# A 16-point transform stage between matmuls: spectrum copied in three pieces, one store buffer more, pauses at block borders, and a weight chunk loaded earlier

## The chip, the cores and the metric

The kernel runs on one core of a Trainium2 chip. Its time is that of one execution on the device, in microseconds (us). TensorE multiplies matrices into PSUM banks, ScalarE and VectorE copy and combine what is there, GpSimd and SyncE mostly issue transfers (DMAs). Each engine works through its own instructions strictly in order.

## What is computed

Four layers run one after the other on a residual x of 2048 rows (S) and 576 channels (D); A mixes by two DFT matrices, B multiplies by a long convolution:

```python
def _A_ref(x, dft_seq_re, dft_seq_im, dft_hid_re, dft_hid_im):
    a = jnp.einsum("bsd,ed->bse", x, dft_hid_re)
    b = jnp.einsum("bsd,ed->bse", x, dft_hid_im)
    return jnp.einsum("ts,bse->bte", dft_seq_re, a) - jnp.einsum("ts,bse->bte", dft_seq_im, b)

def _B_ref(q, k, v, shift_k, ssm_k, ssm_D):
    ...
    kv = k_shift * v                      # k after a causal convolution of 4 taps
    kv_f = rfft(kv padded to 2 * S)       # per channel
    kf_f = rfft(ssm_k padded to 2 * S)
    y = irfft(kv_f * kf_f)[:S]
    return q * (y + kv * ssm_D)

x = x + _A_ref(_layernorm(x), A_dft_...)
x = x + _B_ref(_layernorm(x), B_k, B_v, B_shift_k, B_ssm_k, B_ssm_D)
x = x + _A_ref(_layernorm(x), A_dft_...)
x = x + _B_ref(_layernorm(x), B_k, B_v, B_shift_k, B_ssm_k, B_ssm_D)
```

In B only q depends on x. The convolution result y is the same in both B layers, so the kernel computes it once, beside the first A layer.

## The kernel before

All products are in fp32r. Each operand is split into a rounded high part (ScalarE, a copy) and the rest (VectorE, a subtraction); a product is three matmuls, high x high, high x low and low x high. This pair of instructions is `split` (L91 to L93), and most of the work of ScalarE and VectorE consists of it.

**The first A layer** is `layer` (L292) with 128 steps n: 4 blocks of 512 output rows, in each the real and the imaginary DFT, in each 16 steps k over the rows. A step has 14 matmuls of 512 columns: twelve into four accumulators s and two into a fifth, rm. The DFT matrix for it is loaded two steps ahead on SyncE and split into `cs` (the lines "mats<-flts 128x512" of L92 and L93). At the last k of sixteen, a border, the accumulators are copied out and split into the spectrum u (`evac_u`, `evac_r`). There is one set of accumulators, so the next step's matmuls wait for these copies. At n = 47, 79 and 111 the layer also yields `None` while products of the block before are pending.

**The hidden product** (`hidden`, L268) multiplies the spectrum of a finished block with the hidden DFT matrix W: 27 matmuls of 288 columns, released from their bank by a VectorE addition (L279). W has nine chunks of rows, loaded and split by `load_w` (L217) from step 41 on, two chunks to a step; the ninth has 64 rows of the real and 64 of the imaginary matrix with unlike signs. The first hidden product needs the ninth chunk last.

**The branch** (`branch`, L339) computes the convolution as a long transform in three stages. The middle one, the 16-point stage, has 64 groups. A group's feed is loaded from memory (`flts<-t`) and split (the "mid<-flts 128x576" lines); then come:

- `mid_kernel`: the transform of the convolution kernel, three matmuls into a bank. Partitions 0 to 63 hold the real part, 64 to 127 the imaginary part. ScalarE makes the buffer kk of two halves from it: one copy out of the bank (L496), then three copies of 64 partitions within SBUF (L497 to L499) that put real and imaginary part where the product needs them, one with its sign turned.
- `mid_signal`: the transform of the signal into another bank, and on VectorE the complex product of the two, with the half products in L505, L506 and L507 and their sum in L508. L507 is the last to read the signal's bank.
- `mid_round`: the split of the product (ScalarE "mid<-flts 128x288" and VectorE L492).
- `mid_inverse`, two groups later: three matmuls into a bank, a copy to a store buffer `vo`, a store.

ScalarE's copies of the stage all go through `act` (L483), so the page shows them under one line, L486; the VectorE half of the feed's and the round's split is L492. The last stage of the branch (`i2_products`) reads what the inverse stored, multiplies by a table i2c that GpSimd loads, and stores the result from the same `vo` buffers. All banks of the branch and of the hidden products are three buffers called bk.

**What sets the order.** The program is written as generators that the loop at L733 advances: after each half step of the layer (`whole` False, then True) it takes up to GROUPS = 2 yields of the branch as long as its share of the work is due. Where the work is behind, two yields follow every half step until it has caught up. Within that, the Tile framework's scheduler decides the order of the instructions on each engine and the bank that a product gets. At n = MID_LOAD (44, second half) the branch is advanced once: it lays out the stage's buffers and issues the first two feed loads. The stage's groups run from n = 47 to 103, the last stage's products to 111.

Of the kernel before, what the change touches and what calls it, by code (L numbers as in the profile page):

```python
# [10 lines left out]
F32 = mybir.dt.float32  # L11
FR = mybir.dt.float32r
AF = mybir.ActivationFunctionType
# [20 lines left out]
W_FROM = 41  # L34
HOLD = 125
W_SAVE = 60
MID_LOAD = 44
MID_FROM = 47
I2_END = 111
PREP = 113  # L40
# [25 lines left out]
def fnet_h3_kernel(ctx: ExitStack, tc: tile.TileContext, x, c_mat, w_re, w_im, k_pad, v, shift_k,  # L66
# [24 lines left out]
    def split(h, l, src):  # L91
        a = nc.scalar.activation(h, src, AF.Copy).ins  # L92
        return a, nc.vector.tensor_tensor(l, src, h.bitcast(F32), OP.subtract).ins  # L93

    @contextmanager
    def behind(*instructions):
        with ExitStack() as stack:
            for i in instructions:
                stack.enter_context(tc.issue_after(i))
            yield  # L100

    def split_in(h, l):

        split(h, l, l.bitcast(F32))
# [44 lines left out]

    flts = flat(FLT, F32, "flts")  # L150
    mhalf = flts[:, :1]
    lay(flts, 8, ("stat", STAT, 4))
    lay(flts, RT_AT, ("rt", NT, 1))
    lay(mats, X_END, ("cs", WIDE, 3))
# [9 lines left out]
            nc.gpsimd.dma_start(dst, src)  # L164

    nc.vector.memset(mhalf, -0.5)
    nc.scalar.activation(flts[:, 1:2], mhalf, AF.Copy)

    def norm_stats(src):
# [47 lines left out]
    def load_w():  # L217
        lay(flts, SC_AT + CRAW * NT + 4 * D, ("wl", D, 3))
        wg = region_a(FR, "w").rearrange("p (k n) -> p k n", k=9)
        for ch in range(9):  # L220
            w = two(wg[:, ch])
            raw = ring["wl"]()
            if ch < 8:
                nc.sync.dma_start(raw, (w_re if ch < 4 else w_im)[(ch % 4) * P:(ch % 4 + 1) * P, :])
            else:
                nc.sync.dma_start(raw[:REM], w_re[NC * P:, :])
                nc.sync.dma_start(raw[REM:], w_im[NC * P:, :])
            for lo, hi, sg in ((0, P, 1 if ch < 4 else -1),) if ch < 8 else ((0, REM, 1), (REM, P, -1)):
                if sg > 0:
                    split(w[lo:hi, 0, :], w[lo:hi, 1, :], raw[lo:hi])  # L230
                else:
                    nc.scalar.activation(w[lo:hi, 0, :], raw[lo:hi], AF.Copy, scale=-1.0)
                    nc.vector.scalar_tensor_tensor(w[lo:hi, 1, :], raw[lo:hi], -1.0,
                                                   w[lo:hi, 0, :].bitcast(F32), op0=OP.mult,
                                                   op1=OP.subtract)
            W.append(w)
            yield
        for ch in range(9):
            load_after(w_d[ch], wg[:, ch].bitcast(F32))
            yield  # L240
# [98 lines left out]
    def branch():  # L339
# [126 lines left out]
        at = lay(m1, at, ("yf", D, 2))  # L466
        lay(m1, at, ("fc", 4 * P, 2))
        at = lay(flts, SC_AT + CRAW * NT, ("res", D, 2))
        lay(flts, at, ("land", D, 2), ("kk", D, 2), ("vo", HD, 3), ("p2", HD, 1))
        mc = quads(ring["mc"]())  # L470
        load_fr(mc, midc)
        lo, hi = slice(0, 64), slice(64, 128)
# [10 lines left out]
        def act(*args, **kw):  # L483
            if last_act:
                with tc.issue_after(last_act[-1]):
                    last_act.append(nc.scalar.activation(*args, **kw).ins)  # L486
            else:
                last_act.append(nc.scalar.activation(*args, **kw).ins)
# [4 lines left out]

        def mid_kernel(df):
            pk, kk = mid_half(df, HD), two(ring["kk"]())
            act(kk[:, 0, :], pk[:, :HD], AF.Copy)  # L496
            act(kk[lo, 1, :], kk[hi, 0, :], AF.Copy)  # L497
            act(kk[hi, 1, :], kk[hi, 0, :], AF.Copy, scale=-1.0)
            act(kk[hi, 0, :], kk[lo, 0, :], AF.Copy)  # L499
            return kk  # L500

        def mid_signal(df, kk):
            px = mid_half(df, 0)
            p1, p2 = kk[:, 0, :], ring["p2"]()
            nc.vector.tensor_tensor(p1, px[:, :HD], p1, OP.mult)  # L505
            nc.vector.tensor_tensor(p2[lo], px[hi, :HD], kk[hi, 1, :], OP.mult)  # L506
            nc.vector.tensor_tensor(p2[hi], px[lo, :HD], kk[lo, 1, :], OP.mult)  # L507
            nc.vector.tensor_tensor(p1, p1, p2, OP.add)  # L508
            return p1

# [222 lines left out]
    for n, whole in layer(get_x0, lambda j: x[:, j, :], done0, pending):  # L733
        if (whole or whole is not None and n % J < J - 1) and n <= F1_END:
            at = n if whole else n - 0.5
            at16 = 4 + 2 * F1_16
            want = int(4 + F1_16 * at / 8 if at <= 16 else at16 + (68 - at16) * (at - 16) / (F1_END - 16))
            with behind(made[min(n + 2, J - 1)], *evac):
                while used < want:
                    next(br)  # L740
                    used += 1
        if whole is not None and n >= W_FROM and len(W) < 9:
            with behind(*stored):
                next(wl)
        if whole and n == MID_LOAD:
            next(br)
        if n >= MID_FROM:
            if whole is not None:
                passed += STEP * (4 if whole else 3) / 7 * BORDER.get(n % J, 1.05)
            if whole is None or whole and n % 2 == 1 and n % (2 * J) < J - 1 and pending:  # L750
                finish(pending, 1)
                passed += PIECE
            for _ in range(GROUPS):
                if spent < work * min(1.0, passed / total):
                    with behind(*added, *evac):
                        spent += next(br, work)
# [129 lines left out]
        HU[tb, ch] = t  # L886

    def split_u(tb, ch):
        t = HU[tb, ch]
        for lo, hi, sg in ((0, P, 1 if ch < 4 else -1),) if ch < 8 else ((0, REM, 1), (REM, P, -1)):  # L890
            h, l = t[lo:hi, 0, :], t[lo:hi, 1, :]
            if sg > 0:
                split_in(h, l)
            else:
                raw = l.bitcast(F32)
                nc.scalar.activation(h, raw, AF.Copy, scale=-1.0)
                nc.vector.scalar_tensor_tensor(l, raw, -1.0, h.bitcast(F32), op0=OP.mult, op1=OP.subtract)

    steps = [(tb, m, kp) for tb in range(1, TB) for m in ORDER for kp in range(KP)]
    cs, done = {}, []  # L900
# [205 lines left out]
```

## Time and profile before

| | |
|---|---|
| time, median of 3 runs | 1205.02 us (1201.5, 1205.02 and 1205.65) |
| profiled execution | 1202.6 us, its span on the core 1200.8 us |
| TensorE busy, weight loads busy | 98%, 85% of the span |
| VectorE, ScalarE, GpSimd busy | 70%, 55%, 6% |
| granted TensorE clock | 0.999 |
| DMA | 261.95 MB, 218 GB/s on average |

A row of the profile names the line, the engine, the operation, what it writes and reads, its shape and count, then its busy time in us, the mean in ns of one, and the idle time of the engine just before it with what ended that. PE is TensorE, PEld its weight load, which runs beside the matmul before; DVE is VectorE, ACT ScalarE, POOL GpSimd, SP SyncE. A busy TensorE is not TensorE at its peak, since the ends of matmuls are modelled. In a row of the timeline the first number is the start in us from the span's start, the second the duration.

### The profile page before, as it was taken

How to read it: one execution, taken by the hardware profiler on the slowest of the kernel's cores; microseconds unless marked ns; L12 is line 12 of the kernel's file. 1: busy time of each engine (PE TensorE's matmuls, PEld its weight loads, DVE VectorE, ACT ScalarE, POOL GpSimd, SP SyncE). 2: the span in 40 equal slices, each digit the busy share in tenths (PEclk: the TensorE clock that was granted, in tenths of full speed). 3: DMA queues.
4: the chain of work that ended last, by engine and by line, in shares of the span. 5: the costliest groups of instructions: out<-in, count | busy, mean ns of one | idle time of the engine just before them, and what ended most of it. 6: DMA issues, size and time to landing. Idle time of an engine off the chain costs nothing.

```text
span 1200.8 us, 18269 instructions
## 1 busy us (share of the span) xinstructions
PE 1177.3 (98%) x6320; PEld 1026.5 (85%) x6320; DVE 840.2 (70%) x1498; ACT 665.9 (55%) x1335; POOL 75.3 (6%) x116
## 2 busy tenths in 40 slices
PE   7999999999999999999999999999999999999997
PEld 6878888988888888888988898888888888889997
DVE  7889883679877677675346766775776777774764
ACT  7855665579866678675435566544444445550210
POOL 2210000000000000001101111000000000001111
PEclk9999999999999999999999999999999999999999
DMA  9779898546756667647967686872682677795621
GB/s 363 265 240 311 284 296 259 167 138 182 227 186 183 201 179 227 189 143 235 308 201 242 214 259 218 271 262 77 204 288 79 196 285 266 231 351 148 218 91 40
DMA packets 146110, 261.95 MB, mean 218 GB/s; under 512 B 15841, under 2 KB 44769, under 8 KB 146018
## 3 DMA queue, kind: packets, MB, share of 16 engines
q1 hardware_dynamic: 102674, 205.58, 53.5%
q10 hardware_dynamic: 36432, 42.63, 10.2%
q0 software_dynamic: 6912, 12.59, 4.1%
q8 instruction: 49, 0.80, 0.3%
q14 instruction: 43, 0.35, 0.1%
HBM read 194.09 MB, written 66.65 MB: 217 GB/s over the span
## 4 chain that ended last, share of the span: by engine, by line
PE 80%; ACT 6%; DVE 6%; DMA 4%; issue 2%; POOL 1%; ACTq 0%; SPq 0%; POOLq 0%; DVEq 0%
PE s L75 45%; PE bk L75 30%; PE rm L75 4%; ACT flts L486 3%; DMA flts<-in_c_mat 1%; ACT mid L486 1%; DVE mats L93 1%; DMA flts<-vd 1%; DVE mats L190 1%; DMA t<-flts 1%; ACT mats L92 1%; DMA mid<-in_i2c 1%; DVE f1f L387 1%; POOL flts L616 0%; DVE f1f L382 0%
## 5 line engine op out<-in xcount | busy, mean ns | idle before, releaser
L75 PE MATMUL s<-mats 128*128 128x512 f32 x2088 | 528.5, 391 | 0.8 <-DVE u L93 0.8
L75 PEld LDWEIGHTS s<-mats 128*128 128x128 f32 x2088 | 381.1, 188 | 71.0 <-DVE u L93 1.7
L93 DVE TENSOR_TENSOR mats<-flts,mats 128x512 fp32r<-128x512 f32 x206 | 141.0, 688 | 53.1 <-ACT mats L92 51.5
L92 ACT ACTIVATE mats<-flts 128x512 fp32r<-128x512 f32 x206 | 128.3, 627 | 85.1 <-PE bk L75 31.7
L75 PE MATMUL bk<-mid 128*128 128x288 f32 x768 | 128.1, 298 | 5.3 <-ACT flts L486 2.0
L75 PEld LDWEIGHTS bk<-mid 128*128 128x128 f32 x768 | 114.7, 188 | 20.5 <-ACT flts L486 5.6
L492 DVE TENSOR_TENSOR mid<-flts,mid 128x576 fp32r<-128x576 f32 (+1 forms) x160 | 101.9, 638 | 41.3 <-ACT mid L486 34.4
L75 PE MATMUL bk<-w,u 128*128 128x288 f32 x864 | 121.2, 296 | 1.1 <-DVE flts L279 0.6
L75 PEld LDWEIGHTS bk<-w,u 128*128 128x128 f32 x864 | 117.2, 188 | 5.4 <-DVE flts L279 1.5
L486 ACT ACTIVATE flts<-bk 128x288 f32<-128x288 f32 x160 | 63.0, 405 | 90.6 <-PE bk L75 71.6
L75 PE MATMUL rm<-mats 128*128 128x512 f32 x304 | 95.4, 390 | 0.0
L486 ACT ACTIVATE mid<-flts 128x576 fp32r<-128x576 f32 (+1 forms) x159 | 87.4, 582 | 10.8 <-DMA flts<-vd 7.0
L486 ACT ACTIVATE flts<-flts 64x288 f32<-64x288 f32 x192 | 85.0, 443 | 5.2
L432 ACT ACTIVATE flts<-bk 128x288 f32<-128x288 f32 x128 | 49.5, 410 | 46.4 <-PE bk L75 40.9
L75 PE MATMUL bk<-f1r 128*128 128x288 f32 x384 | 65.0, 301 | 8.1 <-ACT f1r L92 7.7
L75 PEld LDWEIGHTS bk<-f1r 128*128 128x128 f32 x384 | 59.3, 191 | 15.8 <-ACT f1r L92 8.5
L75 PE MATMUL bk<-mats 128*128 128x288 f32 (+1 forms) x376 | 67.8, 317 | 0.0
L75 PEld LDWEIGHTS rm<-mats 128*128 128x128 f32 x304 | 56.9, 188 | 11.8
L75 PE MATMUL s<-t,mats 128*128 128x512 f32 x264 | 64.9, 389 | 0.0
L176 POOL TENSOR_TENSOR flts<-flts 128x1 f32<-128x1 f32 x35 | 29.6, 846 | 523.3 <-DVE flts L175 523.3
L279 DVE TENSOR_TENSOR flts<-flts,bk 128x288 f32<-128x288 f32 x48 | 21.7, 453 | 57.4 <-PE bk L75 57.4
L75 PE MATMUL bk<-mats,t 128*128 128x288 f32 (+1 forms) x368 | 59.3, 303 | 0.0
(143 smaller groups left out, 1491.3 us busy)
## 6 DMA issues: line engine op xcount, KB each, us to landing
flts<-in_c_mat SPq DMA_DIRECT2D x148, 256.0 KB, 3.5
ph<-in_c_mat SPq DMA_DIRECT2D x54, 512.0 KB, 4.1
t<-flts ACTq DMA_DIRECT2D x64, 288.0 KB, 4.5
flts<-t SPq DMA_DIRECT2D x64, 288.0 KB, 3.0
flts<-in_c_mat SPq DMA_DIRECT2D x30, 512.0 KB, 5.2
vd<-flts ACTq DMA_DIRECT2D x64, 144.0 KB, 2.6
flts<-vd SPq DMA_DIRECT2D x32, 288.0 KB, 4.4
mid<-in_i2c POOLq DMA_DIRECT2D x32, 256.0 KB, 5.5
```

The lines of the kernel that those rows point to most:

```text
L75: nc.tensor.matmul(ps, lhsT, rhs, start=first, stop=last, skip_group_check=more)
L92: a = nc.scalar.activation(h, src, AF.Copy).ins
L93: return a, nc.vector.tensor_tensor(l, src, h.bitcast(F32), OP.subtract).ins
L176: pows.append(nc.gpsimd.tensor_tensor(rs, ve, mhalf, OP.pow).ins)
L190: made.append(nc.vector.tensor_tensor(t[:, D + REM:], y[:, :NC * P], h[:, :NC * P], OP.subtract).ins)
L279: added[:] = [nc.vector.tensor_tensor(r[:, cs], r[:, cs], ps[:, :HD], OP.add).ins]
L387: nc.vector.tensor_tensor(rp, rp, out_t, OP.add)
L432: stored[:] = [nc.scalar.activation(so[:, c, :], ps[:, :HD], AF.Copy).ins]
L486: last_act.append(nc.scalar.activation(*args, **kw).ins)
L492: nc.vector.tensor_tensor(l, src, h.bitcast(F32), OP.subtract)
```

## The change

Six edits:

- `mid_kernel` makes kk by three copies of 64 partitions out of the bank, each to its place, and leaves the sign to `mid_signal`. Before it was one copy out of the bank and three within SBUF.
- `mid_signal` writes the crossed half products into the second half of kk instead of a buffer of their own (p2). The first of them is now a three-operand instruction that turns the sign.
- The space of p2 becomes a fourth `vo` buffer.
- In the second half of step n with n % 16 = 14 and the first half of the next, no yield of the branch is taken.
- MID_LOAD is 45: the first feeds are requested behind the ninth chunk of W.
- The chunks with unlike signs (the ninth of W, the ninth of u in the last stage) are split by one pair of instructions over 128 partitions, with a column of +1 and -1 as the scale; before it took two pairs over 64. Two memsets at the start fill that column.

```diff
-MID_LOAD = 44
+MID_LOAD = 45
...
+    def signed_split(h, l, src, sign):
+
+        nc.scalar.activation(h, src, AF.Copy, scale=sign)
+        nc.vector.scalar_tensor_tensor(l, src, sign, h.bitcast(F32), op0=OP.mult, op1=OP.subtract)
...
+    nc.vector.memset(mixed[:REM], 1.0)
+    nc.vector.memset(mixed[REM:], -1.0)
...
-            for lo, hi, sg in ((0, P, 1 if ch < 4 else -1),) if ch < 8 else ((0, REM, 1), (REM, P, -1)):
...
+            if ch < 4:
+                split(w[:, 0, :], w[:, 1, :], raw)
+            else:
+                signed_split(w[:, 0, :], w[:, 1, :], raw, -1.0 if ch < 8 else mixed)
...
-        lay(flts, at, ("land", D, 2), ("kk", D, 2), ("vo", HD, 3), ("p2", HD, 1))
+        lay(flts, at, ("land", D, 2), ("kk", D, 2), ("vo", HD, 4))
...
-            act(kk[:, 0, :], pk[:, :HD], AF.Copy)
-            act(kk[lo, 1, :], kk[hi, 0, :], AF.Copy)
-            act(kk[hi, 1, :], kk[hi, 0, :], AF.Copy, scale=-1.0)
-            act(kk[hi, 0, :], kk[lo, 0, :], AF.Copy)
+            act(kk[lo, 0, :], pk[lo, :HD], AF.Copy)
+            act(kk[hi, 0, :], pk[lo, :HD], AF.Copy)
+            act(kk[hi, 1, :], pk[hi, :HD], AF.Copy)
...
-            p1, p2 = kk[:, 0, :], ring["p2"]()
+            p1, p2 = kk[:, 0, :], kk[:, 1, :]
             nc.vector.tensor_tensor(p1, px[:, :HD], p1, OP.mult)
-            nc.vector.tensor_tensor(p2[lo], px[hi, :HD], kk[hi, 1, :], OP.mult)
-            nc.vector.tensor_tensor(p2[hi], px[lo, :HD], kk[lo, 1, :], OP.mult)
+            nc.vector.scalar_tensor_tensor(p2[lo], px[hi, :HD], -1.0, p2[hi], op0=OP.mult, op1=OP.mult)
+            nc.vector.tensor_tensor(p2[hi], px[lo, :HD], p2[hi], OP.mult)
...
-            for _ in range(GROUPS):
+            near = whole and n % J == J - 2 or whole is False and n % J == J - 1
+            for _ in range(0 if near else GROUPS):
```

The order of the instructions changes from the ninth chunk of W on. TensorE's matmuls before its first hidden product and after the last product of the 16-point stage stand as before.

SyncE's loads around the ninth chunk, before (in_w_re and in_w_im are W, the 64x576 pair its ninth chunk; in_c_mat is the DFT matrix, t_75 a feed, in_x the residual):

```order
L160 DMA flts<-t_75 128x576
L224 DMA flts<-in_w_im 128x576
L160 DMA flts<-in_c_mat 128x512
L224 DMA flts<-in_w_im 128x576
L160 DMA flts<-t_75 128x576
L160 DMA flts<-in_c_mat 128x512
L226 DMA flts<-in_w_re 64x576
L227 DMA flts<-in_w_im 64x576
```

and now, with t_77 the feed:

```order
L166 DMA flts<-t_77 128x576
L232 DMA flts<-in_w_im 128x576
L166 DMA flts<-in_c_mat 128x512
L232 DMA flts<-in_w_im 128x576
L234 DMA flts<-in_w_re 64x576
L235 DMA flts<-in_w_im 64x576
L166 DMA flts<-t_77 128x576
```

The ninth chunk stands ahead of the second feed; the second DFT load of these rows has moved further up, out of this piece.

VectorE in two groups of the 16-point stage behind the first border, before (bk is a bank, 128x288 into mid the round's split, 128x576 the feed's):

```order
L505 TENSOR_TENSOR flts<-bk,flts 128x288
L506 TENSOR_TENSOR flts<-bk,flts 64x288
L507 TENSOR_TENSOR flts<-bk,flts 64x288
L492 TENSOR_TENSOR mid<-flts,mid 128x576
L508 TENSOR_TENSOR flts<-flts 128x288
L93 TENSOR_TENSOR mats<-flts,mats 128x512
L505 TENSOR_TENSOR flts<-bk,flts 128x288
L492 TENSOR_TENSOR mid<-flts,mid 128x288
L506 TENSOR_TENSOR flts<-bk,flts 64x288
L507 TENSOR_TENSOR flts<-bk,flts 64x288
L492 TENSOR_TENSOR mid<-flts,mid 128x576
```

and now:

```order
L508 TENSOR_TENSOR flts<-bk,flts 128x288
L509 SCALAR_TENSOR_TENSOR flts<-bk,flts 64x288
L496 TENSOR_TENSOR mid<-flts,mid 128x288
L510 TENSOR_TENSOR flts<-bk,flts 64x288
L496 TENSOR_TENSOR mid<-flts,mid 128x576
L511 TENSOR_TENSOR flts<-flts 128x288
L93 TENSOR_TENSOR mats<-flts,mats 128x512
L508 TENSOR_TENSOR flts<-bk,flts 128x288
L496 TENSOR_TENSOR mid<-flts,mid 128x288
L509 SCALAR_TENSOR_TENSOR flts<-bk,flts 64x288
L496 TENSOR_TENSOR mid<-flts,mid 128x576
L510 TENSOR_TENSOR flts<-bk,flts 64x288
```

The round's split stands between the half products in both; in the second group the feed's split now stands ahead of the last half product (L510, formerly L507), which is the last to read the signal's bank.

TensorE at the border at n = 79, from the hidden product on, before (w,u is the hidden product, mid the branch, s and rm the layer):

```order
L75 MATMUL bk<-w,u 128x288 x27
L75 MATMUL bk<-mid 128x288 x6
L75 MATMUL s_66<-mats 128x512
L75 MATMUL bk<-mid 128x288 x9
L75 MATMUL s_66<-mats 128x512 x2
L75 MATMUL s_67<-mats 128x512 x3
L75 MATMUL bk<-mid 128x288 x3
L75 MATMUL s_68<-mats 128x512 x2
L75 MATMUL bk<-mid 128x288
L75 MATMUL s_68<-mats 128x512
L75 MATMUL s_69<-mats 128x512 x3
```

and now:

```order
L75 MATMUL bk<-w,u 128x288 x27
L75 MATMUL bk<-mid 128x288 x9
L75 MATMUL s_66<-mats 128x512 x2
L75 MATMUL bk<-mid 128x288 x3
L75 MATMUL s_66<-mats 128x512
L75 MATMUL s_67<-mats 128x512 x3
L75 MATMUL s_68<-mats 128x512 x3
L75 MATMUL s_69<-mats 128x512 x3
L75 MATMUL rm<-mats 128x512 x2
```

Branch matmuls no longer stand between the layer's matmuls in the second part of the step; they follow behind the border.

More of the change, by code (lines that the diff above doesn't have):

```diff
@@ L151, in fnet_h3_kernel @@
     mhalf = flts[:, :1]
+    mixed = flts[:, 2:3]
     lay(flts, 8, ("stat", STAT, 4))
@@ L227, in load_w @@
                 nc.sync.dma_start(raw[REM:], w_im[NC * P:, :])
-            for lo, hi, sg in ((0, P, 1 if ch < 4 else -1),) if ch < 8 else ((0, REM, 1), (REM, P, -1)):
[L229 to L235, printed above, removed]
+            if ch < 4:
+                split(w[:, 0, :], w[:, 1, :], raw)
+            else:
+                signed_split(w[:, 0, :], w[:, 1, :], raw, -1.0 if ch < 8 else mixed)
             W.append(w)
@@ L888, in split_u @@
     def split_u(tb, ch):
[L889 to L897, printed above, removed]
+        h, l = HU[tb, ch][:, 0, :], HU[tb, ch][:, 1, :]
+        if ch < 4:
+            split_in(h, l)
+        else:
+            signed_split(h, l, l.bitcast(F32), -1.0 if ch < 8 else mixed)
     steps = [(tb, m, kp) for tb in range(1, TB) for m in ORDER for kp in range(KP)]
```

## The prediction, made before the changed kernel was run

> **What bounds the kernel now.** I read the stretches first, since the change touches one of them, then who waited for whom in it. The columns are the stretch, its length and the busy time of TensorE, its weight loads, VectorE, ScalarE and GpSimd, with their instructions in brackets.
>
> ```profile
> 214.00:441.00 227.00, 223.86 (x1315) 198.72 (x1314) 169.88 (x336) 167.88 (x366) 2.12 (x4) 1.00 0.60 181
> 441.00:617.00 176.00, 172.50 (x973) 151.74 (x972) 108.33 (x197) 111.54 (x238) 13.79 (x26) 1.00 0.71 217
> ```
>
> TensorE is busy for 223.86 of 227 us and for 172.50 of 176. The 16-point stage lies in these 403 us, and the change moves matmuls nowhere else and takes none away. A gain can come only out of TensorE's stalls here. The waits of the weight loads (PEld), then of the matmuls (PE), over the same 403 us (total, times, longest):
>
> ```profile
> PEld bk L75 <- ACT flts L486: 6.9, 16, 1.3
> PEld bk L75 <- DVE flts L507: 3.7, 7, 0.9
> PEld bk L75 <- DVE flts L279: 2.1, 4, 0.7
> PEld bk L75 <- DVE w L233: 0.7, 1, 0.7
> PEld s L75 <- DVE u L93: 0.7, 1, 0.7
> PEld bk L75 <- DVE mid L492: 0.4, 2, 0.2
> ```
>
> ```profile
> PE bk L75 <- ACT flts L486: 2.0, 4, 0.9
> PE bk L75 <- DMA mid<-in_i2c: 1.7, 1, 1.7
> PE bk L75 <- DVE flts L507: 1.3, 4, 0.4
> PE bk L75 <- DVE flts L279: 0.9, 3, 0.4
> PE bk L75 <- DVE w L233: 0.5, 1, 0.5
> PE s L75 <- DVE u L93: 0.2, 1, 0.2
> ```
>
> Without the wait for the i2c load, the weight loads waited 14.5 us and the matmuls 4.9. Neither is what TensorE lost: a load runs ahead of its matmul, and a late matmul still counts some waiting as busy. One stall gives the scale:
>
> ```profile
> 371.97 1.53 PE L75 MATMUL s<-mats 128*128 128x512 f32 x6
> 373.34 0.62 PE L75 MATMUL rm<-mats 128*128 128x512 f32 x2
> 374.58 1.53 PE L75 MATMUL s<-mats 128*128 128x512 f32 x6
> 376.56 0.82 PEld L75 LDWEIGHTS bk<-mid 128*128 128x128 f32 x6 [0.87 <-ACT flts L486]
> 376.56 1.06 PE L75 MATMUL bk<-mid 128*128 128x288 f32 x6 [0.45 <-ACT flts L486]
> ```
>
> Six layer matmuls undisturbed take 371.97 to 373.34, 1.37 us to the next start; the same six before the stall take 374.58 to 376.56, 1.98. So 0.61 was lost where PEld says 0.87 and PE 0.45. With 0.61/0.87 = 0.70 the 14.5 become 10.2 us; with 0.61/0.45 = 1.36 the 4.9 become 6.7. Many waits show on the loads alone, so I take 10.2. That is all the change can win; the i2c wait (1.7) is outside it, since its load waits for products whose order near there is unchanged. The span can't fall below about 1190.
>
> **The change, part by part.** *Spectrum pieces.* Costs on ScalarE and VectorE (busy, mean ns):
>
> ```profile
> L486 ACT ACTIVATE flts<-flts 64x288 f32<-64x288 f32 x192 | 85.0, 443 | 5.2
> L486 ACT ACTIVATE flts<-bk 128x288 f32<-128x288 f32 x160 | 63.0, 405 | 90.6 <-PE bk L75 71.6 <-ACT flts L486 5.0 <-DMA yb<-flts 4.7
> L486 ACT ACTIVATE mid<-flts 128x288 fp32r<-128x288 f32 x64 | 28.5, 445 | 1.7 <-DVE flts L508 0.2
> ```
>
> ```profile
> L492 DVE TENSOR_TENSOR mid<-flts,mid 128x576 fp32r<-128x576 f32 x96 | 72.7, 758 | 29.8 <-ACT mid L486 23.4 <-DMA yb<-flts 2.7 <-PE bk L75 1.3
> L506 DVE TENSOR_TENSOR flts<-bk,flts 64x288 f32<-64x288 f32 x64 | 29.4, 459 | 1.8
> L492 DVE TENSOR_TENSOR mid<-flts,mid 128x288 fp32r<-128x288 f32 x64 | 29.2, 457 | 11.5 <-ACT mid L486 11.0
> L507 DVE TENSOR_TENSOR flts<-bk,flts 64x288 f32<-64x288 f32 x64 | 28.8, 451 | 0.9
> L233 DVE SCALAR_TENSOR_TENSOR w<-flts,w 64x576 fp32r<-64x576 f32 x1 | 0.8, 756 | 0.0
> ```
>
> Before, a group spends 405 + 3 x 443 = 1734 ns on them. A 64x288 piece out of a bank is not in the trace. Half the partitions cost what all do (443 against 445, both out of SBUF), and 288 columns out of a bank cost 405; 443 is the other end. At 405 the three pieces take 1215: 519 ns less, 64 x 0.519 = 33 us less ScalarE work (26 at 443). ScalarE is off the path most of the time, so this is no gain by itself; what counts is when a bank comes free. On VectorE the first half product becomes the three-operand form; at 576 columns that takes 756 against 758 for the two-operand one, so it costs nothing.
>
> VectorE's longest wait in the stage is for these copies; ScalarE's own splits of the DFT halves (L92) wait for the layer's step before:
>
> ```profile
> DVE flts L505 <- ACT flts L486: 40.4, 36, 2.7
> ```
>
> ```profile
> ACT mats L92 <- PE rm L75: 10.9, 16, 2.0
> ```
>
> I follow one group by hand. Its spectrum was ready at 369.60:
>
> ```profile
> 369.60 0.41 ACT L486 ACTIVATE flts<-bk 128x288 f32<-128x288 f32 x1 [3.22 <-PE bk L75]
> 370.04 1.37 ACT L486 ACTIVATE flts<-flts 64x288 f32<-64x288 f32 x3
> 371.44 0.46 DVE L505 TENSOR_TENSOR flts<-bk,flts 128x288 f32<-128x288 f32 x1 [1.79 <-ACT flts L486]
> 372.87 0.45 DVE L507 TENSOR_TENSOR flts<-bk,flts 64x288 f32<-64x288 f32 x1
> ```
>
> L505 waited for the last of four copies; now it needs two pieces, so it may start at 369.60 + 2 x 0.405 = 370.41, 1.03 earlier. The signal's bank is released by the last half product, at 372.87 + 0.45 = 373.32 before. In the new order the round's split (L492, 128x288) comes ahead of that product, and its ScalarE half (445) stands behind the third piece: 369.60 + 1.215 + 0.445 = 371.26; then 0.457 for its VectorE half and 0.451 for the product: 372.17, 1.15 earlier. That is the good case. Counted in the new order, in 17 of the 64 groups a half product (0.459) and the next feed's split (0.758) stand between as well: 373.39, no gain. In 14, ScalarE has the split of a DFT half (L92) directly ahead of the pieces; as that waits for the step before, they gain nothing or lose. So 33 to 47 of 64 win; I take 35, 55%. The spectrum's own bank loses: it was free at 370.01 and is now at 370.82, 0.81 later.
>
> The waits on L486 and L507 are 0.70 x (6.9 + 3.7) = 7.4 us. 55% of it is 4.1; for the later spectrum bank I give back 0.9 (one wait of 0.81 and its follower; nothing if no bank is short, 64 x 0.81 = 52 if every one were): **-3.2**. Bounds: 52 - 7.4 = +45, and -7.4.
>
> *Hidden product's bank.* 0.70 x 2.1 = 1.5 us were lost to L279, late because VectorE was still at a group's products, which now start earlier. I take half, **-0.7** (0 to -1.5).
>
> *W's last chunk.*
>
> ```profile
> 215.93 0.67 ACT L92 ACTIVATE w<-flts 64x576 fp32r<-64x576 f32 x1
> ```
>
> ```profile
> 210.99 0.57 SPq L226 DMA_DIRECT2D flts<-in_w_re  x1
> ```
>
> ```profile
> 218.25 0.53 PE L75 MATMUL bk<-w,u 128*128 128x288 f32 x2 [0.49 <-DVE w L233]
> ```
>
> The chunk's load stood behind a feed load and a DFT load on SyncE (issued at 210.99), its splits began at 215.93, and the last of the four ended just ahead of 218.25. Now its load is ahead of the second feed, the DFT load has moved further up, and two splits of 128 partitions replace four of 64: one ScalarE step (0.67) and one of VectorE (0.756, at L233) less. The wait, 0.70 x 0.7 = 0.5, goes: **-0.5** (0 to -0.7). Behind the chunk the second feed now queues, two issues of 0.57 later; the matmuls of its group come after a whole hidden product, which hides that, and without this cover the second group starts 1.1 late. The merged splits in the last stage feed matmuls that wait for none of them: 0. The two memsets at the start come while VectorE waits for the first input: 0.
>
> ```profile
> 3.69 0.82 DVE L173 BATCH_NORM_STATS2 flts<-early 128x6 f32<-128x288 f32 x2 [2.82 <-DMA early<-in_x]
> ```
>
> *Branch pause.* At 516 us a block's spectrum was evicted under branch work:
>
> ```profile
> 516.27 1.91 PEld L75 LDWEIGHTS s<-mats 128*128 128x128 f32 x9 [0.68 <-DVE u L93]
> ```
>
> That 0.70 x 0.7 = 0.5 goes, **-0.5**. The skipped half steps' products come later, two to a half step until caught up; in such a stretch ScalarE and VectorE are busiest, and I charge **+0.4** (0 to +2, two waits as long as the longest PE one).
>
> *Fourth store buffer.* It ends ScalarE's waits for stores:
>
> ```profile
> ACT flts L486 <- DMA yb<-flts: 4.7, 4, 2.4
> ACT flts L486 <- DMA vd<-flts: 3.0, 2, 2.4
> ```
>
> These six fall largely where TensorE waits for i2c or not at all: **0** (to -0.5).
>
> Sum: -3.2 - 0.7 - 0.5 - 0.5 + 0.4 = -4.5. The profiled execution took 1202.6 (1200.8 of span and 1.8 around it), so 1198.1 of that kind. It lies 2.4 below the median of the three runs, 1205.02; one of them lies lower still, at 1201.5, two at 1205. I add two thirds of the 2.4, which makes 1204.2 the base of all times below, and predict 1204.2 - 4.5 = **1199.7**, 0.44% under the median. A difference of under 0.5%, 6 us, a measurement of this kernel can't tell from none; faster begins at 1199.0.
>
> **The rivals.** *Nearly all bank waits go*: the 31 groups without a gain don't decide, since the next claim on their bank comes late enough. Then -7.4 - 1.5 - 0.5 - 0.5 = -9.9 at most, -6.6 with two thirds of it: 1194.3 to 1197.6. For it speaks that L505 starts up to 1.03 earlier and the longest single wait on L486 is 1.3; against it that the new order puts more work ahead of the releasing product. 24%.
>
> *The pieces lie off the path*: bank waits move and don't shrink; W and the border alone give -1.0, 1203.2. So it also looks if the fewer and shorter steps only lengthen ScalarE's idle time. 13%.
>
> *Slower: the spectrum's bank decides.* Spectrum, signal, inverse and hidden products share three banks. If the one held 0.81 longer is the next one claimed in 14 of 64 groups, that is 11.3; less 1.0 elsewhere, +10.3: 1214.5. It is slower by over 0.5% (1211.05) from ten such groups on (10 x 0.81 - 1.0 = 7.1). Against it: in the group above the bank is free at 370.82, and the layer matmuls at 371.97 still stand ahead of the next claim but one. 7%. The Trainium skill, Perfetto Trace Analysis, "Optimization Strategy", says that a gap which keeps coming back on the engine that should be full can mean that there isn't enough PSUM for the next tile. The sixteen waits on L486 agree with it so far as they are waits for banks; whether holding one bank longer adds to them no run here shows yet.
>
> **How the numbers follow.** Forecast 56%, all bank waits 24%, off the path 13%, slower 7%. The likeliest gives 1199.7. The range, 1194.0 to 1205.5, holds the first rival, the second, and the forecast with its smaller terms at their ends (-0.7, -1.5, +2); it leaves out the slower rival and the far ends of the bank term. Faster by over 0.5%: 24%, and 13% from forecasts that come out more than 0.7 better than the middle, 0.37; slower 0.07; the rest 0.56.
>
> **What would show it.** Right: ScalarE's busy time in the stage down by some 30 us, L505's wait for ScalarE (40.4 us) mostly gone, no TensorE wait for W, TensorE waits on the spectrum and signal banks about halved. Wrong: those waits as long as before with other releasers (the pieces' line, the feed's split), or a new wait behind a border, around 250 to 280 us or 440 to 460 us, where the paused work is caught up; or a difference outside the stage.

## The result, and the profile after

The changed kernel took 1200.07 us (median of 14 runs, 1197.45 to 1201.04), the kernel before 1202.26 beside it: a ratio of 0.9978, with a 95% interval of 0.9970 to 0.9987. One of the 14 executions of the kernel before took 6704.54 us and is left out of the ratio. Measured once more it was 1199.36 against 1201.20, ratio 0.9985 (0.9977 to 0.9993). So by the ratios it is faster by 1.8 to 2.7 us, under the 0.5% that the prediction counts as a difference; the forecast was 1199.7 and "no difference". With so many runs the measurement tells more than the prediction granted it: both intervals leave out 1. The profiled execution took 1199.98, its span 1198.1, against 1202.6 and 1200.8.

The two stretches after the change, with the columns as before (length, then busy TensorE, weight loads, VectorE, ScalarE, GpSimd):

```profile
214.00:441.00 227.00, 224.74 (x1319) 199.49 (x1318) 170.59 (x333) 147.92 (x321) 2.12 (x4) 1.00 0.60 181
441.00:617.00 176.00, 173.90 (x989) 153.71 (x988) 109.73 (x199) 103.42 (x219) 13.75 (x26) 1.00 0.72 217
```

ScalarE is busy for 251.3 us of the 403 instead of 279.4, 28 less, somewhat less than the 33 forecast (some 30 where the prediction says what would show it). VectorE's busy time stays at 278 to 280 us. The waits of the weight loads in these 403 us (total, times, longest):

```profile
PEld bk L75 <- ACT flts L490: 8.7, 16, 1.4
PEld bk L75 <- DVE flts L510: 2.0, 5, 0.6
PEld bk L75 <- DVE flts L283: 1.8, 3, 0.9
PEld s L75 <- DVE u L93: 0.6, 1, 0.6
```

L490 and L510 are the old L486 and L507. Their waits are 10.7 us, before 10.6: nothing was halved; the weight moved from the signal's last product (3.7 to 2.0) to ScalarE's copies (6.9 to 8.7). A second profile of the changed kernel has 7.6 + 2.0 = 9.6. The wait for the i2c load, which the forecast had put outside the change, is gone: no such row is left. Elsewhere the copies did what was intended. The groups of the pieces and of the first two half products, and VectorE's and ScalarE's waits:

```profile
L490 ACT ACTIVATE flts<-bk 64x288 f32<-64x288 f32 x192 | 77.6, 404 | 46.7 <-PE bk L75 29.9 <-DVE flts L510 6.4 <-DVE mid L496 3.0
L509 DVE SCALAR_TENSOR_TENSOR flts<-bk,flts 64x288 f32<-64x288 f32 x64 | 29.4, 460 | 1.7
L508 DVE TENSOR_TENSOR flts<-bk,flts 128x288 f32<-128x288 f32 x64 | 29.1, 455 | 24.4 <-ACT flts L490 14.4 <-PE bk L75 9.8
```

```profile
ACT mats L92 <- PE rm L75: 24.3, 29, 2.0
```

A piece takes 404 ns and the three-operand product 460, as assumed (405, 459). VectorE's wait for the spectrum fell from 40.4 to 14.4 us. ScalarE now idles for the layer's step before for 24.3 us instead of 10.9: about half of the 28 us of shorter work went into this idle time.

The waits of the weight loads are not what TensorE loses, so I also took every start of a matmul in the stage, here from the first matmul of the first hidden product to the start of the one behind the last branch product. I subtracted the undisturbed interval (131 ns for 288 columns, 227 for 512) and summed what lies over it by what released the stall. Stalls of less than some 0.08 us are in no column. ScalarE's stalls are told apart by the copy that ended them: one for the kernel's spectrum, or one for an inverse or last-stage product (a 128x288 copy followed by a store). In us, one profiled execution each; "behind" and "one copy" are kernels of the experiments:

| kernel | length of the stage | i2c load | inverse copies | spectrum copies | last half product | hidden product | W |
|---|---|---|---|---|---|---|---|
| before | 401.62 | 1.90 | 2.65 | 0.50 | 1.90 | 1.52 | 0.76 |
| changed | 398.72 | 0 | 3.79 | 1.36 | 1.11 | 1.32 | 0 |
| changed, again | 398.09 | 0.26 | 2.65 | 1.38 | 1.09 | 1.45 | 0 |
| pieces alone | 400.49 | 0 | 2.45 | 1.44 | 1.97 | 0.75 | 1.16 |
| pause alone | 398.97 | 1.77 | 2.69 | 0.13 | 0.62 | 1.01 | 0.40 |
| W alone | 401.41 | 1.48 | 2.08 | 0.53 | 1.97 | 2.45 | 0.81 |
| all but pieces | 400.19 | 2.10 | 2.54 | 0.80 | 0.62 | 1.77 | 0 |
| all but pause | 398.59 | 0 | 1.76 | 1.59 | 1.97 | 1.46 | 0 |
| three store buffers | 398.05 | 0 | 3.45 | 1.37 | 1.11 | 1.27 | 0 |
| short i2c load | 399.33 | 0 | 2.15 | 0.51 | 1.88 | 1.26 | 1.11 |
| splits behind | 398.57 | 0 | 2.49 | 1.30 | 1.17 | 2.27 | 0.56 |
| one copy | 396.07 | 0 | 2.27 | 0.13 | 1.05 | 1.18 | 0 |
| one copy, no pause | 395.77 | 0.12 | 0.37 | 0 | 2.87 | 1.18 | 0 |
| one copy, behind | 396.03 | 1.17 | 2.37 | 0 | 0.58 | 0.55 | 0 |

Undisturbed, the 1389 matmuls of 288 columns and the 889 of 512 would take 383.8 us. What a kernel's stage has beyond this and its columns is 7.0 to 9.0 us, made of many small stalls. The profile names no releaser for the 0.26 and the 0.12 in the i2c column; they end within 0.15 us after such a load landed. The stage became 2.9 us shorter (3.5 in the second profile): 1.9 by the i2c load, 0.8 by W, 0.8 by the last half product, 0.2 by the hidden product and 1.2 of the small ones; 0.9 went back to the spectrum copies, and the inverse copies cost 1.1 more in one profile and nothing in the other.

### The profile page after: what moved, and what is told of

Read it like the earlier page. It is cut to its first block, busy times and chain, and to the rows that moved or that the text cites. A ratio compares the mean times of both kernels' runs of the same rounds, so it can differ in the third digit from the quotient of the medians.

```text
span 1198.1 us, 18264 instructions
## 1 busy us (share of the span) xinstructions
PE 1177.1 (98%) x6320; PEld 1026.9 (86%) x6320; DVE 838.9 (70%) x1495; ACT 633.9 (53%) x1266; POOL 75.1 (6%) x116
## 4 chain that ended last, share of the span: by engine, by line
PE 71%; ACT 3%; DVE 3%; DMA 2%; issue 1%; ACTq 0%; POOLq 0%; DVEq 0%
PE s L75 39%; PE bk L75 28%; PE rm L75 4%; ACT flts L490 2%; ACT mid L490 1%; DMA flts<-in_c_mat 1%; DVE mid L496 1%; DMA flts<-t 1%; DMA flts<-vd 1%; DVE u L93 1%; DMA ph<-in_c_mat 0%; DVE mats L93 0%; ACT mats L92 0%; DVE flts L510 0%; DVE flts L269 0%
## 5 line engine op out<-in xcount | busy, mean ns | idle before, releaser
L490 ACT ACTIVATE flts<-bk 64x288 f32<-64x288 f32 (+1 forms) x288 | 115.9, 406 | 103.1 <-PE bk L75 85.0
L490 ACT ACTIVATE mid<-flts 128x576 fp32r<-128x576 f32 (+1 forms) x159 | 87.1, 581 | 14.9 <-DMA flts<-vd 9.6
L436 ACT ACTIVATE flts<-bk 128x288 f32<-128x288 f32 x128 | 49.0, 410 | 46.5 <-PE bk L75 39.2
L283 DVE TENSOR_TENSOR flts<-flts,bk 128x288 f32<-128x288 f32 x48 | 21.8, 453 | 63.8 <-PE bk L75 63.6
L75 PEld LDWEIGHTS bk<-mats 128*128 128x128 f32 x376 | 55.6, 188 | 3.4
```

What stands on the lines that cost most here:

```text
L75: nc.tensor.matmul(ps, lhsT, rhs, start=first, stop=last, skip_group_check=more)
L283: added[:] = [nc.vector.tensor_tensor(r[:, cs], r[:, cs], ps[:, :HD], OP.add).ins]
L436: stored[:] = [nc.scalar.activation(so[:, c, :], ps[:, :HD], AF.Copy).ins]
```

## The experiments

**Theories.** A: the pieces only move TensorE's waits for banks, and the gain is the small edits'. B: the pieces are the gain, and another edit gives some back. Four kernels take the change apart. *Pieces alone*: the kernel before with this edit and three store buffers.

```diff
-            act(kk[:, 0, :], pk[:, :HD], AF.Copy)
-            act(kk[lo, 1, :], kk[hi, 0, :], AF.Copy)
-            act(kk[hi, 1, :], kk[hi, 0, :], AF.Copy, scale=-1.0)
-            act(kk[hi, 0, :], kk[lo, 0, :], AF.Copy)
+            act(kk[lo, 0, :], pk[lo, :HD], AF.Copy)
+            act(kk[hi, 0, :], pk[lo, :HD], AF.Copy)
+            act(kk[hi, 1, :], pk[hi, :HD], AF.Copy)
```

> The kernel before with the three pieces and the half products in kk alone (three store buffers, no pause, first feeds at 44, W split as before). Theory A, the pieces only shift TensorE's waits for banks (10.6 us of weight-load waits on the spectrum's and signal's readers before, 10.7 after): within 0.7 us of before, with those waits still 9 to 12 us. Theory B, the pieces are the gain and another edit gives some of it back: 2.5 to 4 us faster than before, with those waits under 8 us.

Measured: 1199.49 against 1201.30, ratio 0.9986 (0.9976 to 0.9997), 1.8 us faster. Its weight loads waited:

```profile
PEld bk L75 <- ACT flts L486: 7.6, 19, 1.3
PEld bk L75 <- DVE flts L506: 3.8, 9, 0.8
```

L506 is the last half product here. The two make 11.4 us, as much as A expects, and yet the kernel is faster than A allows. Its profile has no wait for i2c. (The profiled execution took 1204.41, 4.9 over its median; 3.5 of that came ahead of the stage, where the kernels are alike.)

*All but the pieces* keeps the other edits, the first half of kk being made as before:

```diff
-            act(kk[lo, 0, :], pk[lo, :HD], AF.Copy)
-            act(kk[hi, 0, :], pk[lo, :HD], AF.Copy)
-            act(kk[hi, 1, :], pk[hi, :HD], AF.Copy)
+            act(kk[:, 0, :], pk[:, :HD], AF.Copy)
+            act(kk[lo, 1, :], kk[hi, 0, :], AF.Copy)
+            act(kk[hi, 1, :], kk[hi, 0, :], AF.Copy, scale=-1.0)
+            act(kk[hi, 0, :], kk[lo, 0, :], AF.Copy)
```

> The changed kernel with the four copies and p2 of before (so three store buffers again); pause, later first feeds and merged splits stay. Theory A: 1.5 to 2.5 us faster than before, like the whole change. Theory B: between 0.5 us faster and 1 us slower than before.

Measured: 1200.35, ratio 0.9992 (0.9981 to 1.0002): 1 us faster by the medians, between the two, with an interval that includes no difference. The i2c wait is there:

```profile
PE bk L75 <- DMA mid<-in_i2c: 1.9, 1, 1.9
```

*Pause alone*:

```diff
-            for _ in range(GROUPS):
+            near = whole and n % J == J - 2 or whole is False and n % J == J - 1
+            for _ in range(0 if near else GROUPS):
```

> The kernel before with the pause at the borders alone. Theory A: within 0.7 us of before: the wait for the spectrum's eviction at 516 us (0.5 us) goes and one behind another border comes. Theory B: 1 to 2 us slower, through bank waits behind the borders where the work is caught up.

Measured: 1199.94, ratio 0.9986 (0.9977 to 0.9996), 1.4 us faster. Both theories missed. The border at 516 us is a small part of it (0.4 us lost there before). The pause shifts all groups behind a border against the layer's steps, and four stalls on the signal's last product (before at 336, 347, 388 and 490 us, 1.90 us in all) go; two new ones, at 258 and 448 us, cost 0.62:

```profile
PEld bk L75 <- ACT flts L486: 6.5, 17, 1.0
PEld bk L75 <- DVE flts L507: 1.1, 2, 0.6
PE bk L75 <- DMA mid<-in_i2c: 1.6, 1, 1.6
```

1.1 instead of 3.7 in L507, and the i2c wait as before.

*W alone*: the kernel before with the earlier ninth chunk and the merged splits. Of the two edits the first reads:

```diff
-MID_LOAD = 44
+MID_LOAD = 45
```

> The kernel before with the first feeds requested at step 45 and the merged splits of the chunks with unlike signs alone. Both theories: 0.5 to 1.0 us faster, since the wait for W's last chunk at 218 us (0.7 on the weight load, 0.9 us with the matmul behind it) is gone, and nothing else moves.

Measured: 1200.96, ratio 0.9996 (0.9988 to 1.0005): no difference that shows. The wait for W (L105 is now its split, L283 the addition that frees the hidden product's bank) stays:

```profile
PEld bk L75 <- DVE flts L283: 3.0, 4, 1.1
PEld bk L75 <- DVE w L105: 0.7, 1, 0.7
```

In ScalarE's timeline of this kernel and of the changed one, the splits of the last two chunks of W, released by their loads:

```profile
214.94 0.69 ACT L104 ACTIVATE w<-flts 128x576 fp32r<-128x576 f32 x1 [1.69 <-DMA flts<-in_w_im]
216.65 0.78 ACT L104 ACTIVATE w<-flts 128x576 fp32r<-128x576 f32 x1 [1.02 <-DMA flts<-in_w_im]
```

```profile
213.78 0.69 ACT L104 ACTIVATE w<-flts 128x576 fp32r<-128x576 f32 x1 [1.29 <-DMA flts<-in_w_im]
215.10 0.78 ACT L104 ACTIVATE w<-flts 128x576 fp32r<-128x576 f32 x1 [0.64 <-DMA flts<-in_w_im]
```

The ninth chunk is split when its transfer lands, and here it landed 1.2 us later than in the changed kernel with the same edit, counted from the first hidden matmul (214.23 here, 213.90 there). ScalarE still waits for it, so the landing is the limit, not its place behind other loads alone. The chunk's second load was issued at 211.61 us before, 209.13 in the changed kernel and 210.36 here, and took 4.3, 5.9 and 6.2 us to land: most of the earlier issue was lost to a longer transfer. At the hidden product's bank, freed by L283, 2.45 us were lost here and 1.52 before.

**Second round.** The pieces alone give 1.8 us and the pause alone 1.4, and the whole change no more than 1.8 to 2.7. Four variants of the changed kernel, beside 1201.53 for the kernel before. *Three store buffers*:

```diff
-        lay(flts, at, ("land", D, 2), ("kk", D, 2), ("vo", HD, 4))
+        lay(flts, at, ("land", D, 2), ("kk", D, 2), ("vo", HD, 3))
```

> The changed kernel with three store buffers in place of four. Buffers off the path (the prediction's term of 0): ScalarE waits for stores of some 5 to 8 us come back, the time stays within 0.5 us of the changed kernel (1200.07), and the i2c load is waited for no more than in the changed kernel. Rival, the fourth buffer is what lets the branch's end be reached early enough for the i2c load: a TensorE wait for that load of 1 to 2 us comes back, and the time is 1 to 2 us longer.

Measured: 1198.16, ratio 0.9973 (0.9961 to 0.9984), the same as with four within the intervals, and no i2c wait. No effect of the fourth buffer shows, and it is not what removes the wait. Of ScalarE's waits for stores only 1.6 us come back, not 5 to 8; of the 7.7 us before, most went with something else than the buffer.

*All but the pause*:

> The changed kernel without the pause of the branch ahead of a border. Theory A (the gain is of the pause; the pieces only move the bank waits): 1 to 1.7 us slower than the changed kernel, with TensorE's waits for the signal's last product up by 1 us. Theory B (the pieces gain, the catch-up behind a border gives some back): 0.5 to 1.5 us faster than the changed kernel, without the 1.35 us stall at 457 us.

Measured: 1198.84, ratio 0.9978 (0.9967 to 0.9989): neither. Beside the pieces no effect of the pause shows on balance:

```profile
PEld bk L75 <- ACT flts L490: 6.5, 16, 1.0
PEld bk L75 <- DVE flts L510: 3.8, 9, 0.8
```

Without it the waits are 6.5 + 3.8, with it 8.7 + 2.0 (7.6 + 2.0 in the second profile). What the pause saves at the signal's last product comes back at ScalarE's copies. That two groups follow each other in the catch-up may be the reason; no run here singles it out. The longest stall of the changed kernel, at 457 us behind the border of n = 79, is not the pause's, though: it stands at 456.41 here with 0.94 us, and in the kernel before at 457.69 with 1.02. In the changed kernel, ScalarE around it:

```profile
456.23 0.68 ACT L490 ACTIVATE mid<-flts 128x576 fp32r<-128x576 f32 x1 [1.73 <-DMA flts<-vd]
456.93 1.12 ACT L490 ACTIVATE flts<-bk 128x288 f32<-128x288 f32 x3
```

```profile
457.40 0.40 PE L75 MATMUL bk<-mid 128*128 128x288 f32 x1 [1.19 <-ACT flts L490]
```

A split waits 1.73 us for a feed that is read back (vd), and the copies out of the banks stand behind it in ScalarE's order, which the helper `act` fixes; TensorE waits for the first of them.

*One copy*: the spectrum leaves its bank in one copy, and two copies within SBUF place it. The bank is free after 0.41 instead of 1.25 us.

```diff
-            act(kk[lo, 0, :], pk[lo, :HD], AF.Copy)
-            act(kk[hi, 0, :], pk[lo, :HD], AF.Copy)
-            act(kk[hi, 1, :], pk[hi, :HD], AF.Copy)
+            act(kk[:, 0, :], pk[:, :HD], AF.Copy)
+            act(kk[hi, 1, :], kk[hi, 0, :], AF.Copy)
+            act(kk[hi, 0, :], kk[lo, 0, :], AF.Copy)
```

> The changed kernel with the spectrum copied out of its bank in one copy of all 128 partitions, and two copies of 64 behind it that place the halves: the bank is free some 0.8 us earlier, and the placed spectrum is ready some 0.1 us later than with three pieces. If the longer hold of the spectrum's bank gives back what the earlier products win: weight loads' waits on the spectrum and signal banks fall from 10.7 us to under 7, and the time is 1.5 to 3 us shorter. If the hold doesn't decide (the waits are for the signal's bank): waits between 9 and 12 us, time within 0.7 us of the changed kernel.

Measured: 1197.68, ratio 0.9963 (0.9951 to 0.9976), 3.9 us faster than before by the medians; the stage is 2.0 to 2.7 us shorter than the changed kernel's.

```profile
PEld bk L75 <- ACT flts L490: 5.6, 14, 0.8
PEld bk L75 <- DVE flts L510: 2.6, 7, 0.5
```

8.2 us of waits: not under 7, but the fall is where it was expected, at ScalarE's copies. In the changed kernel such a stall reads (ScalarE's three pieces, then TensorE):

```profile
514.09 1.25 ACT L490 ACTIVATE flts<-bk 64x288 f32<-64x288 f32 x3
515.39 0.66 PE L75 MATMUL bk<-mid 128*128 128x288 f32 x3 [0.33 <-ACT flts L490]
```

The bank is free when the third piece ends at 515.34, and the next matmul into it starts 0.05 later, 0.49 after its undisturbed time. With one copy the stalls at spectrum copies drop from 1.36 to 0.13 us. Those at inverse copies are 2.27, against 3.79 and 2.65 in the two profiles of the changed kernel.

*Splits behind*: VectorE's splits come behind the last half product of the group ahead, so that nothing delays the release of the signal's bank.

```diff
-            nc.vector.tensor_tensor(l, src, h.bitcast(F32), OP.subtract)
+            with behind(*freed):
+                nc.vector.tensor_tensor(l, src, h.bitcast(F32), OP.subtract)
...
-            nc.vector.tensor_tensor(p2[hi], px[lo, :HD], p2[hi], OP.mult)
+            freed[:] = [nc.vector.tensor_tensor(p2[hi], px[lo, :HD], p2[hi], OP.mult).ins]
```

> The changed kernel, with VectorE's splits of the next round and feed ordered behind the last half product of the group ahead, so that nothing stands before the signal bank's release. If the splits ahead of the release (the prediction's 17 groups) keep the waits up: weight loads' waits on the spectrum and signal banks fall from 10.7 us to under 7 and the time is 1 to 3 us shorter. If they don't decide, or the splits that come later are waited for in their place: bank waits 9 us or more, or new waits of TensorE for the split of the feed (mid), and the time within 1 us or longer.

Measured: 1196.77 (5 runs), ratio 0.9958 (0.9946 to 0.9971). It is faster than the kernel before, but its trace doesn't show why. L511 is the last half product here; the bank waits are 9.1 us, the stage 398.57, no shorter than the changed kernel's, and the profiled execution took 1198.94, the slowest of its five.

```profile
PEld bk L75 <- ACT flts L490: 7.5, 15, 1.3
PEld bk L75 <- DVE flts L511: 1.6, 3, 0.8
```

**Third round**, beside 1201.20 for the kernel before. *The changed kernel again* gave the second profile of the table.

> The changed kernel once more, with a second profile beside the other kernels of this call. If the picture of the first profile is of the kernel and not of one execution: 2 to 3 us faster than before, weight loads' waits on the spectrum and signal banks of 10 to 11.5 us, no TensorE wait for the i2c load, and one wait of over 1 us at about 457 us. If the i2c wait went by chance: a wait of 1 to 2 us for that load at about 558 us.

Measured: 1199.36, 1.8 us faster, a little less than expected; waits of 7.6 + 2.0 = 9.6 us, below the 10 expected, and 0.26 us lost to an i2c load, not 1 to 2. The stall at 457 us lost 0.64 us instead of 1.35, with ScalarE waiting 1.01 us for the feed instead of 1.73: it goes with when the feed lands.

*Short i2c load*, in the kernel before:

```diff
-        def load_fc(k):
+        def load_fc(k, n=P):
             if k < len(rows):
                 fcs[k] = quads(ring["fc"]())
-                load_fr(fcs[k], i2c[rows[k]])
+                load_fr(fcs[k][:n], i2c[rows[k]][:n])
...
-                    load_fc(used + ahead + m)
+                    load_fc(used + ahead + m, 32 if m == 0 else P)
```

> The kernel before, with nothing of the change; of the one i2c load that TensorE waited for, only 32 of its 128 partitions are loaded, so that part of one product is computed from old values. If the pieces' gain is that this load is no longer waited for: the wait of 1.7 to 1.9 us at 561 us goes, and the time is 1.3 to 2.2 us shorter than before, as much as with the pieces alone (ratio 0.9986). If that wait only uncovers the next load's, or another cause stands behind the pieces' gain: under 0.6 us shorter.

Measured: 1199.62, ratio 0.9985 (0.9976 to 0.9994), 1.6 us faster, with three quarters of one load left out and nothing else. The wait is gone, and the gain is the same as of the pieces alone (0.9986) and of the changed kernel beside it (0.9985). So within the interval the wait is worth its full length on the clock, and no other wait takes it over. One thing the form doesn't separate: the feed (vd) requested 0.6 us behind this load lands earlier, too, 4.3 us after its issue instead of 6.1; in the changed kernel it is 3.9. That load, from its issue to its landing (KB, us), in the kernel before, with the pause alone, in the changed kernel and in the short form:

```profile
mid<-in_i2c POOLq DMA_DIRECT2D x1, 256.0 KB, 6.5
```

```profile
mid<-in_i2c POOLq DMA_DIRECT2D x1, 256.0 KB, 6.4
```

```profile
mid<-in_i2c POOLq DMA_DIRECT2D x1, 256.0 KB, 3.8
```

```profile
mid<-in_i2c POOLq DMA_DIRECT2D x1, 64.0 KB, 4.1
```

TensorE wants it some 4.8 us after the issue (6.5 less a wait of 1.7, 6.4 less 1.6; the three other kernels that waited give 4.8 as well). In the four kernels with the old copies and the whole load it took 6.1 to 6.7 us, in nine profiles with the pieces or the one copy 3.6 to 5.8; one copy with splits behind had 5.8 and waited 1.0. What makes it land earlier is not settled. One difference shows: the DFT matrix's load is issued 1.3 us ahead of it in the kernel before and 1.8 in the changed one (SyncE's and GpSimd's issues).

```profile
553.32 0.33 SPq L160 DMA_DIRECT2D flts<-in_c_mat  x1
554.65 0.53 POOL L164 DMA_DIRECT2D mid<-in_i2c  x1 [47.77 <-PE bk L75]
```

```profile
551.59 0.33 SPq L166 DMA_DIRECT2D flts<-in_c_mat  x1
553.40 0.53 POOL L170 DMA_DIRECT2D mid<-in_i2c  x1 [47.60 <-PE bk L75]
```

This lead goes with the landing in all thirteen profiles that load the whole of it. It is 1.3 us in the four with the old copies (landing after 6.1 to 6.7), 1.55 in one copy with splits behind (5.8), and 1.8 to 2.4 in the other eight (3.6 to 4.7). The feed load just ahead of the DFT load comes earlier with it, 2.8 instead of 2.3 us ahead of the i2c load in the two kernels shown. Whether this half microsecond is the cause wasn't tried.

Last, two combinations. *One copy and splits behind*:

> The changed kernel with both edits: the spectrum out of its bank in one copy, and VectorE's splits behind the signal's last product. If the two act on different waits (the spectrum bank's release, the signal bank's release): 2.5 to 4 us faster than the changed kernel, weight loads' waits on the two banks under 7 us. If they take away the same waits: within 0.7 us of the better of the two (ratio to the kernel before 0.996).

Measured: 1197.94, ratio 0.9970 (0.9959 to 0.9981): the second case, or less. The waits are 9.2 us, and i2c is waited for again (1.0).

*One copy, no pause*:

> The changed kernel with the spectrum out of its bank in one copy and without the pause of the branch. If the pause costs as much behind the border as it saves ahead of it: within 0.7 us of the same kernel with the pause (ratio to the kernel before 0.9963), with the waits for the signal's last product up by about 1 us and those for ScalarE's copies down by as much. If the pause gains by itself once the spectrum bank is free early: 1 to 2 us slower than with it.

Measured: 1196.71, ratio 0.9966 (0.9955 to 0.9976), the same as with the pause, and the exchange is the one expected, larger:

```profile
PEld bk L75 <- DVE flts L510: 5.3, 12, 1.2
PEld bk L75 <- ACT flts L490: 2.8, 10, 0.5
```

One copy beats the kernel before by about 4 us, with the pause and without it (3.9 and 4.5 by the medians, 4.4 and 4.1 by the ratios). Over the changed kernel the second is ahead by 2.7 us on the same chip (1196.71 against 1199.36, 12 runs each). The first ran beside the form with three store buffers, and there the gap was 0.5 (1197.68 against 1198.16, five and six runs); so how much one copy gains over the pieces is known only to lie between these, while the stages of all three profiles with it are the shortest.

## Why the forecast held, and where it failed

The time, 1199.7, was within 0.4 us of both measurements, and that was luck: two errors cancelled. The base of 1204.2 was 2 to 3 us too high (the kernel before has a median of 1201.2 to 1202.3 over many runs; of the three shown, 1201.5 was the typical one). The gain of 4.5 us was 1.8 to 2.7 us too large, and the largest part of what was gained came from a wait that the forecast had left out. Of the signs of being right that the prediction named, ScalarE's shorter work and the missing wait for W came; L505's wait fell by two thirds; the bank waits were not halved. Its sign of being wrong came, too: waits as long as before, at the pieces' line, and new stalls behind a border, between 258 and 283 us. By its steps:

- *Spectrum pieces, -3.2.* This is the step that failed: the runs show 0 to +1.2 for it by the table's bank columns. The lengths (405, 459), ScalarE's shorter work and L505's earlier start were right. The term -4.1 was wrong in two ways. The scale of 0.70, taken from one stall, made 7.4 us of the 10.6 us of waits; the starts give 5.06 for L486 and L507 together. And the share of 55%, counted for the release of the *signal's* bank, was applied to all of it, while L486 stands for three sorts of copies: of its 3.16 us, 2.65 are copies of inverse or last-stage products, which no earlier half product releases. The stall from which the scale was taken was itself one of these: in ScalarE's timeline a store follows the copy.

```profile
376.12 0.39 ACT L486 ACTIVATE flts<-bk 128x288 f32<-128x288 f32 x1
376.54 0.33 ACTq L523 DMA_DIRECT2D vd<-flts  x1
```

  Open to the argument were the 1.90 us of L507 alone. They became 1.11, but 1.97 with the pieces alone and 1.97 in the changed kernel without the pause: the pieces took nothing away, and the fall came with the pause. The +0.9 for the bank held longer was right in size (0.50 to 1.36), though spread over five stalls and not one wait and its follower.
- *The i2c wait, "outside the change".* Wrong, and worth 1.6 to 1.9 us. The order of its products is unchanged, as said; but the wait depends on when the load lands, and that went from 6.5 to 3.8 us after the issue. The loads issued ahead of it on SyncE did move, by half a microsecond.
- *Hidden product's bank, -0.7.* It gave 0.1 to 0.2. The two largest stalls are now at 219 and 225 us, behind the chunk of W.
- *W's last chunk, -0.5.* The wait of 0.76 went in the changed kernel, but not with this edit alone, where it stayed and cost more behind it; on the clock it gives 0.3 us, with an interval that includes no difference.
- *Branch pause, -0.5 and +0.4.* The sum was right beside the pieces (0), the reason not: alone it gives 1.4 us, with 1.3 us less of stalls at the signal's last product. The border wait itself shows again at 258 us (0.6 us of a weight load's wait).
- *Fourth store buffer, 0; merged splits of the last stage, 0; memsets, 0.* Nothing contradicts them; only the first was tested.
- *The rivals.* "The pieces lie off the path" describes the banks best: their waits moved and didn't shrink. It gave the change 1.0 us, and the kernel gained 1.8 to 2.7; the i2c wait, which this rival leaves out as well, can account for the rest. "Nearly all bank waits go" didn't happen. "The spectrum's bank decides" named a real mechanism, 0.9 us where it put 11.3; one copy takes it away. The rule of the Trainium skill, Perfetto Trace Analysis, "Optimization Strategy", that a recurring gap can mean too little PSUM, agrees with this: a bank freed 0.84 us earlier (1.25 less 0.41) made the stage 2.0 to 2.7 us shorter.

## What to carry to other kernels

A row of waits names a line, not a cause: before a share is multiplied on it, split its stalls by which instruction ended each and which buffer that freed. Splitting a copy into pieces shortened here what waits for the data (40.4 to 14.4 us at L505) and lengthened what waits for the source (0.50 to 1.36); where banks are short, try to free the bank in one copy and rearrange in SBUF. A transfer whose landing ends a wait belongs to the terms even if nothing about it is changed: here it landed 3.8 instead of 6.5 us after its issue, and the wait that went with it was the largest part of the gain.

## What the runs showed of the hardware

A ScalarE copy of 64x288 out of a bank takes 404 ns and one of 128x288 405; out of SBUF they take 443 and 445. Half the partitions save nothing. The Trainium skill, Perfetto Trace Analysis, "Optimizing Scalar/DVE Operations", gives ScalarE an overhead of about 93 ns on SBUF and 51 on PSUM, 42 apart, and says that the profiled latency is about twice that. The mean times here differ by 39 to 40 ns, which agrees with the figures as they stand and not with twice their difference.

Unexpected was how little a load's size says about when it lands: 256 KB of i2c landed after 3.6 to 6.7 us in the same place of the program, a quarter of it after 4.1. The Trainium skill, DMA: Bandwidth & Descriptors, "Issuing engines are not separate DMA queues", says that transfers of all queues interleave on the same engines; that fits, though no run here separates it from other causes.
